# First stage in the order of a written table, small VectorE scalings into padded rows, small doubles zeroed by a bound

## The chip, the cores and the metric

The kernel runs on one core of a Trainium2 chip. A core has a matrix engine (PE, its weight loads PEld), VectorE (DVE), ScalarE (ACT), GpSimd (POOL) and a sync engine (SP) that here only starts transfers. Each engine takes its instructions in program order and waits on semaphores for the others. The metric is the device time of the whole program in microseconds, the median of three runs; beside it stands one profiled execution, from which all durations below come.

## What is computed

There are three layers, one behind the other, over batch 4, sequence 576 and width 512 (8 heads of 64). Only the first and part of the second concern this change.

```python
# layer 1, per batch and head: attention over means of 4 positions, repeated, plus a local band
q_d = q.reshape(B, H, Sd, factor, D).mean(axis=3)        # the same for k and v; factor 4
out_d = sm_attn(q_d, k_d, v_d)                           # softmax attention of 144 x 144
out_up = np.repeat(out_d, factor, axis=2)
mask = np.abs(pos[:, None] - pos[None, :]) < factor      # band of +-3 positions
...                                                      # softmax of the masked scores
return (out_up + out_local).astype(np.float32)
# layer 2: a token mixer and a channel mixer, both relu(x @ w1) @ w2 added to x
h = np.maximum(xt @ w_tok1, 0.0) @ w_tok2
u = x + h.transpose(0, 2, 1)
h2 = np.maximum(u @ w_ch1, 0.0) @ w_ch2
# layer 3: four causal attention experts with a top-2 gate
```

The four weights of layer 2 arrive as 64-bit floats, and the kernel turns them into 32-bit floats on the chip.

## The kernel before, in words

**Stages.** The first stage is layer 1 and the token mixer. The second is the channel mixer: 1440 matmuls into the tile `c`, with the weights converted as it goes. The third is layer 3. The change rewrites the first stage, and one step of the weight conversion that the second stage runs too.

**Units and halves.** Layer 1 is cut into 16 units (batch, pair of heads). A unit has its own steps, each a small function: `q` and `v` load; `qd`, `kd`, `pv` take the sums of four; `sl` (PE) makes the local scores in PSUM, `mx` (DVE) their negated maximum and its scaling by 0.125, `ex` (ACT) ten exponentials with their sums, `rs` (DVE) the reciprocal of the sums, `P` (POOL) the product; `tl` (PE) turns P, `tc` (ACT) copies it out, `ol` (PE) multiplies by v. The pooled attention has the parallel steps `sd`, `md`, `ed`, `rd`, `Pd`, `pdt`, `pc`, `pod`, `oc`. `ad` (DVE) adds the two results into U. After two units a half (batch, half of the width) can run the token mixer: `tx`, `xh`, `xl`, `h`, `hh`, `hl`, `pu`, `ua`. Thirteen weight tiles have the steps `w` (load), `g` (ACT: absolute value of the high word), `t` (ACT: low word), `a`, `f`, `gd` (DVE: shift and mask, join, zero where small), `add` (POOL), `hi` (ACT), `lo` (DVE).

**Order.** The 717 steps of the first stage are emitted in one list, and this list is the order on every engine. Before, `arrange` makes the list while the program is built: it takes, step by step, the one that its table of costs (`COST`) and ranks (`RANK`) puts first. Up to the last unit or weight step the list is emitted alone; the rest (49 steps of the halves) is spread over the first three rounds of the second stage. Two PSUM buffers of two banks serve `sl` and `sd`, so a `sl` or `sd` waits for the `ex` or `ed` two places earlier.

**The small scalings.** Per unit VectorE runs four of them, on 128x10 or 72x4 numbers, all from SBUF to SBUF and each a contiguous row: in `mx` (L463, tile `nmx`), `md` (L493, `nd`), `rs` (L476) and `rd` (L505). ACT's exponentials take `nmx` and `nd` as their bias; POOL's products take `rs` and `rd`.

Of the kernel before, what the change touches and what calls it, by code (L numbers as in the profile page):

```python
# [55 lines left out]
NU, NH, NC = B * NP, 2 * B, 7 + 2 * JG  # L56
COST = dict(
    lq=0.55, qd=0.76, kd=1.45, pv=2.1, sl=1.85, mx=1.0, ex=2.95, rs=0.42, P=1.26, sd=0.65, md=0.95, ed=1.42,
    rd=0.5, Pd=1.14, pdt=0.45, pc=0.7, tl0=0.35, tc0=0.5, tl1=0.23, tc1=0.42, pod=0.55, oc=0.3, ol0=0.55, ad0=0.39,
    ol1=0.8, ad1=0.52, tx0=0.43, xh0=0.62, xl0=0.69, tx1=0.43, xh1=0.62, xl1=0.69, tx2=0.2, xh2=0.38, xl2=0.42,  # L60
    h0=1.7, h1=1.7, hh=0.63, hl=0.66, pu=0.8, ua=0.46, g=0.67, t=0.6, a=0.43, f=0.69, gd=0.68, add=1.26, hi=0.65,
    lo=0.68
)
RANK = dict(
    q=-25.9, v=-9.3, qd=-32.3, kd=45.9, pv=5.7, sl=2.5, mx=-0.7, ex=-25.2, rs=-61.0, P=-3.5, sd=-14.1, md=24.9,
    ed=-0.7, rd=7.4, Pd=-19.3, pdt=-18.8, pc=-3.7, tl=-11.3, tc=-14.7, pod=32.5, oc=-21.4, ol=-13.1, ad=18.2,
    tx=58.0, xh=5.8, xl=-59.2, h=48.8, hh=-16.2, hl=-11.1, pu=63.2, ua=-1.9, w=-38.0, g=44.1, t=9.8, a=11.8,
    f=-11.1, gd=2.5, add=-22.3, hi=5.3, lo=-8.5
)
HELD = dict(b1=ABANKS[0], b2=ABANKS[1], q=3, k=KB, z=KB, vz=VB, vp=1, vd=3, qd=3, kd=3, P=3, Pd=2, PdT=2, PT=2, OdT=2,  # L70
            xh0=1, xh1=1, xh2=1, hh=1, raw=2, w=2)
CONV = (2.8, 11.1, 37.6, 17.7)
SLACK = 0.17


def rank(step, i):
    if step in ("w", "g", "t", "a", "f", "gd", "add", "hi", "lo"):
        c0, cs, d0, ds = CONV
        return (c0 + cs * i if i < 7 else d0 + ds * (i - 7)) + RANK[step]
    return (20 * i + 10 if step in ("tx", "xh", "xl", "h", "hh", "hl", "pu", "ua") else 10 * i) + RANK[step]  # L80


def first_stage():

    ops = {}

    def op(step, i, eng, deps=(), held=(), sub=None, cost=None, after=()):
        cost = COST[step + ("" if sub is None or step + str(sub) not in COST else str(sub))] if cost is None else cost
        ops[step, i, sub] = (eng, cost, deps, held, after, rank(step, i))

    for i in range(NU):
        op("q", i, "SP", cost=[288, 144, 144, 288], after=[("q", i - 1, None)],
           held=[("q", [("sl", i, None), ("qd", i, None)]), ("z", [("sl", i, None)]), ("k", [("kd", i, None)])])
        op("v", i, "SP", cost=[160, 160, 336], after=[("v", i - 1, None)],
           held=[("vz", [("ol", i, 1)]), ("vp", [("pv", i, None)])])
        op("qd", i, "DVE", [("q", i, None)], [("qd", [("sd", i, None)])])
        op("kd", i, "POOL", [("q", i, None)], [("kd", [("sd", i, None)])])
        op("pv", i, "POOL", [("v", i, None)], [("vd", [("pod", i, None)])])
        op("sl", i, "PE", [("q", i, None)], [("b2", [("ex", i, None)])], after=[("tl", i - 3, 1)])
        op("mx", i, "DVE", [("sl", i, None)])  # L100
        op("ex", i, "ACT", [("mx", i, None)], [("P", [("tl", i, 1)])])
        op("rs", i, "DVE", [("ex", i, None)])
        op("P", i, "POOL", [("rs", i, None)])
        op("sd", i, "PE", [("qd", i, None), ("kd", i, None)], [("b2", [("ed", i, None)])], after=[("pdt", i - 2, None)])
        op("md", i, "DVE", [("sd", i, None)])
        op("ed", i, "ACT", [("md", i, None)], [("Pd", [("pdt", i, None)])])
        op("rd", i, "DVE", [("ed", i, None)])
        op("Pd", i, "POOL", [("rd", i, None)])
        op("pdt", i, "PE", [("Pd", i, None)], [("b1", [("pc", i, None)])], after=[("pod", i - 2, None)])
        op("pc", i, "ACT", [("pdt", i, None)], [("PdT", [("pod", i, None)])])  # L110
        op("tl", i, "PE", [("P", i, None)], [("b1", [("tc", i, 0)])], 0, after=[("ol", i - 2, 1)])
        op("tc", i, "ACT", [("tl", i, 0)], [("PT", [("ol", i, 1)])], 0)
        op("tl", i, "PE", [("tl", i, 0)], [("b1", [("tc", i, 1)])], 1)
        op("tc", i, "ACT", [("tl", i, 1), ("tc", i, 0)], [], 1)
        op("pod", i, "PE", [("pc", i, None), ("pv", i, None)], [("b1", [("oc", i, None)])], after=[("ad", i - 2, 1)])
        op("oc", i, "ACT", [("pod", i, None)], [("OdT", [("ad", i, 1)])])
        op("ol", i, "PE", [("tc", i, 1), ("v", i, None), ("pod", i, None)], [("b1", [("ad", i, 0)])], 0)
        op("ad", i, "DVE", [("ol", i, 0), ("oc", i, None)], [], 0)
        op("ol", i, "PE", [("ol", i, 0)], [("b1", [("ad", i, 1)])], 1)
        op("ad", i, "DVE", [("ol", i, 1), ("ad", i, 0)], [], 1)  # L120
    for k in range(NH):
        for g in range(3):
            op("tx", k, "PE", [("ad", 2 * k, 1), ("ad", 2 * k + 1, 1)], [("b1", [("xl", k, g)])], g,
               after=[("h", k - 1, 1)])
            op("xh", k, "ACT", [("tx", k, g)], [(f"xh{g}", [("h", k, 1)])], g)
            op("xl", k, "DVE", [("xh", k, g)], [], g)
        op("h", k, "PE", [("xl", k, g) for g in range(3)] + [("lo", x, None) for x in range(3)],
           [("b1", [("hl", k, None)])], 0, after=[("pu", k - 1, 3)])
        op("h", k, "PE", [("h", k, 0)], [], 1)
        op("hh", k, "ACT", [("h", k, 1)], [("hh", [("pu", k, 3)])])  # L130
        op("hl", k, "DVE", [("hh", k, None)])
        for j in range(4):
            op("pu", k, "PE", [("hl", k, None)] + [("lo", x, None) for x in range(3, 7)] + ([("pu", k, j - 1)] if j else []),
               [("b1", [("ua", k, j)])], j)
            op("ua", k, "DVE", [("pu", k, j)], [], j)
    for x in range(NC):
        z = 1 if x < 2 or x > 6 else 0.5 if x == 2 else 0.6
        op("w", x, "SP", cost=[128 if x == 2 else 512 * z], after=[("w", x - 1, None)],
           held=[("raw", [("f", x, None), ("t", x, None), ("g", x, None)])])
        for step, eng, deps, held in (("g", "ACT", ["w"], [("w", [("lo", x, None), ("hi", x, None)])]),  # L140
                                      ("t", "ACT", ["w", "g"], []), ("a", "DVE", ["w", "g"], []), ("f", "DVE", ["a"], []),
                                      ("gd", "DVE", ["f"], []), ("add", "POOL", ["gd", "t"], []),
                                      ("hi", "ACT", ["add"], []), ("lo", "DVE", ["hi"], [])):
            op(step, x, eng, [(d, x, None) for d in deps], held, cost=COST[step] * z)
    return ops


def arrange(ops):

    end, order, todo = {}, [], dict(ops)  # L150
    free = dict(PE=4.0, ACT=1.0, DVE=3.0, POOL=4.0, SP=0.6)
    held = {k: [] for k in HELD}
    wire, window, warm, busy = 0.0, 0, True, 0.0
    while todo:
        can = []
        for n, (eng, cost, deps, hold, after, r) in todo.items():
            waits = [q for tag, rd in hold if len(held[tag]) >= HELD[tag] for q in held[tag][-HELD[tag]]]
            if any(d not in end for d in deps) or any(d in todo for d in after) or any(q not in end for q in waits):
                continue
            t = max([free[eng]] + [end[d] + (0.09 if ops[d][0] != eng else 0) for d in deps] + [end[q] + 0.09 for q in waits])  # L160
            can.append((t, r, n))
        t, r, n = min(can)
        eng = ops[n][0]
        t, r, n = min((c for c in can if ops[c[2]][0] == eng and c[0] <= t + SLACK), key=lambda c: (c[1], c[0]))
        eng, cost, deps, hold, after, r = todo.pop(n)
        order.append(n)
        if eng == "SP":
            for kb in cost:
                t += 0.5
                wire = max(wire, t + 1.0) + kb * 0.00366  # L170
            free[eng], end[n] = t, wire + 0.9
        else:
            if eng == "PE":
                while t >= (window + 1) * 3.413:
                    warm = busy >= (0.66 if warm else 0.93) * 3.413
                    window, busy = window + 1, 0.0
# [897 lines left out]
```

## Time and profile before

| | us |
|---|---|
| three runs | 713.15, 714.07, 717.11 (median 714.07) |
| the profiled execution | 715.17 |
| its span from the first to the last instruction | 713.4 |
| PE busy in the span | 657.8 (92%) |
| DVE busy | 476.4 (67%) |
| ACT busy | 384.5 (54%) |
| POOL busy | 168.8 (24%) |

The shares are means over three stages that differ: the first stage ends near 190 us, the channel mixer near 508 us. In the first stage PE, DVE, ACT and POOL all work at 64 to 80%. A stretch has to be read by itself.

### The profile page before, as it was taken

The page shows a single profiled execution, that of the slowest core. Times are in us where ns is not written, and L with a number is a line of the kernel's source. Part 1 is how long each engine was busy: PE and PEld are TensorE (multiplying, and loading weights), DVE is VectorE, ACT ScalarE, POOL GpSimd, SP SyncE. Part 2 cuts the span into 40 slices and gives each one's busy share as a digit, 9 for nine tenths or more (in the row PEclk, how much of TensorE's full clock was granted, in tenths as well). Part 3 has the DMA queues.
Part 4 walks back from the last instruction along what each step waited for, and adds up shares of the span by engine and source line. Part 5 has one row for each costly group of instructions (what it writes and reads, how often), then busy time and mean ns, then how long its engine had stood idle before and what let it go on. Part 6 is the DMA issues. An engine that isn't in the chain of part 4 may idle for free.

```text
span 713.4 us, 13279 instructions
## 1 busy us (share of the span) xinstructions
PE 657.8 (92%) x4844; PEld 580.6 (81%) x4844; DVE 476.4 (67%) x1156; ACT 384.5 (54%) x1229; POOL 168.8 (24%) x204
## 2 busy tenths in 40 slices
...
GB/s 251 212 233 183 263 253 179 138 89 40 1 1 29 139 40 60 88 1 5 54 60 1 0 45 16 0 1 1 5 63 26 11 78 50 23 87 34 34 31 103
DMA packets 31760, 52.24 MB, mean 73 GB/s; under 512 B 3728, under 2 KB 16528, under 8 KB 31696
## 3 DMA queue, kind: packets, MB, share of 16 engines
...
q8 instruction: 38, 0.62, 0.4%
...
## 4 chain that ended last, share of the span: by engine, by line
PE 75%; DVE 10%; ACT 8%; POOL 3%; DMA 3%; issue 2%; ACTq 0%; POOLq 0%; DVEq 0%
PE c L222 42%; PE proj L222 7%; PE vp L222 4%; PE o L222 4%; PE wo L222 3%; PE s L222 3%; ACT P L471 3%; PE pt L225 3%; PE h L222 2%; PE pu L222 2%; DMA vp<-in_vp_dram 1%; PE sl L222 1%; DMA qT<-in_qT_dram 1%; ACT PT L901 1%; PE ol L222 1%
## 5 line engine op out<-in xcount | busy, mean ns | idle before, releaser
L257 ACT ACTIVATE hh<-c 128x460 fp32r<-128x460 f32 (+1 forms) x60 | 33.1, 552 | 109.6 <-PE c L222 109.1
L222 PE MATMUL c<-hl,wch 128*128 128x460 f32 (+1 forms) x240 | 89.4, 373 | 0.0
L222 PE MATMUL c<-uh,wcl 128*128 128x460 f32 (+1 forms) x240 | 89.2, 372 | 0.0
L222 PE MATMUL c<-ul,wch 128*128 128x460 f32 (+1 forms) x240 | 89.1, 371 | 0.0
L222 PE MATMUL c<-uh,wch 128*128 128x460 f32 (+1 forms) x240 | 89.1, 371 | 0.0
L222 PE MATMUL c<-hh,wcl 128*128 128x460 f32 (+1 forms) x240 | 89.1, 371 | 0.0
L222 PE MATMUL c<-hh,wch 128*128 128x460 f32 (+1 forms) x240 | 89.0, 371 | 0.0
L266 DVE SCALAR_TENSOR_TENSOR hl<-c,hh 128x460 fp32r<-128x460 f32 (+1 forms) x60 | 38.1, 635 | 59.6 <-ACT hh L257 59.5
L340 POOL TENSOR_TENSOR wc_t<-wc_f,wc_t 128x512 int32<-128x512 int32 x24 | 33.4, 1397 | 175.3 <-ACT wc_t L328 156.4
L680 ACT ACTIVATE uh<-u 128x460 fp32r<-128x460 f32 (+1 forms) x80 | 46.3, 586 | 28.3 <-PE c L222 19.0
L681 DVE TENSOR_TENSOR ul<-u,uh 128x460 fp32r<-128x460 f32 (+1 forms) x80 | 49.8, 634 | 8.0 <-ACT uh L680 8.0
L471 ACT ACTIVATE P<-sl,nmx 128x64 f32<-128x64 f32 x160 | 47.5, 338 | 10.8 <-DVE nmx L463 8.5
L876 ACT ACTIVATE Pc<-Pc,nm 112x576 f32<-112x576 f32 (+4 forms) x80 | 46.8, 588 | 10.0 <-DVE nm L875 9.8
L875 DVE CUSTOM_DVE_ANT_0 Pc<-s,caus 112x576 f32<-112x576 f32 (+4 forms) x80 | 40.8, 517 | 13.2 <-PE s L222 12.0
L222 PEld LDWEIGHTS c<-hh,wch 128*128 128x128 f32 x240 | 45.2, 188 | 5.4
L222 PEld LDWEIGHTS c<-uh,wch 128*128 128x128 f32 x240 | 45.1, 188 | 5.2
L222 PEld LDWEIGHTS c<-uh,wcl 128*128 128x128 f32 x240 | 45.1, 188 | 5.2
L222 PEld LDWEIGHTS c<-ul,wch 128*128 128x128 f32 x240 | 45.1, 188 | 5.2
L222 PEld LDWEIGHTS c<-hh,wcl 128*128 128x128 f32 x240 | 45.1, 188 | 5.1
L222 PEld LDWEIGHTS c<-hl,wch 128*128 128x128 f32 x240 | 45.1, 188 | 5.1
L222 PE MATMUL s<-K,Q 128*112 128x288 f32 (+3 forms) x192 | 42.3, 321 | 3.0 <-DVE Q L268 1.3
L792 POOL MEMSET L<- 116x20 f32 x4 | 0.4, 119 | 170.8 <-DVE u L704 132.5
...
## 6 DMA issues: line engine op xcount, KB each, us to landing
...
```

The source lines that it names most:

```text
L222: behind(nc.tensor.matmul(*a, **kw))
L225: behind(nc.tensor.transpose(*a))
L257: nc.scalar.activation(hi, src, AF.Relu if relu else AF.Copy, **({"scale": scale} if scale else {}))
L266: nc.vector.scalar_tensor_tensor(lo, src, 0.0, h, op0=OP.max, op1=OP.subtract)
L340: nc.gpsimd.tensor_tensor(t, r["f"], t, op=OP.add)
L471: nc.scalar.activation(P[:, t, h], r["sl"][:, bk, j], AF.Exp, bias=r["nmx"][:, bk, j:j + 1], scale=0.125, accum_out=sm[:, t, h:h + 1])
L680: nc.scalar.activation(hi, u, AF.Copy)
L681: getattr(nc, ULO).tensor_tensor(lo, u, hi.bitcast(F32), op=OP.subtract)
L792: nc.gpsimd.memset(ST[b]["L"], 0.0)
L875: nc.vector.tensor_tensor_reduce(pv_, sv, mask, -1.0, 3.0e38, OP.add, OP.min, nm[:nq])
L876: nc.scalar.activation(P[:nq, :n], P[:nq, :n], AF.Exp, bias=nm[:nq], scale=-1.0, accum_out=su[:nq])
L901: nc.scalar.activation(PT[:TQ].rearrange("p (c q) -> p c q", q=S)[:, :m, t * TQ:t * TQ + nq], v[:TQ, :m], AF.Copy)
```

## The change

It has three parts, and 717 steps as before.

1. `arrange` with its costs and ranks is gone. The list of steps stands in the program as a table, `STEPS`; its first words are in the diff below.
2. The four small scalings write rows of 3 of which 2 are used (5 rows for `nmx` and `rs`, 3 rows for `nd` and `rd`), from a contiguous row of 10 or 6. The maxima go into a row of their own first (`nraw`, and one shared `NR`). The sums of `ed` go into three fixed tiles `SR`. Four memsets on POOL fill these tiles once.
3. In the weight conversion `gd` now comes ahead of `a`: it raises the absolute value to at least 2^-15 in place (one input) instead of multiplying the joined word by a comparison (two inputs), and `a` shifts that value instead of the raw high word.

```diff
-    steps = arrange(first_stage())
+    steps = []
+    for word in STEPS.split():
+        step = word.rstrip("0123456789.")
+        i, _, sub = word[len(step):].partition(".")
+        steps.append((step, int(i), int(sub) if sub else None))
...
+STEPS = """
+    q0 kd0 qd0 w0 g0 sl0 q1 gd0 t0 mx0 sd0 a0 w1 f0 md0 v0 ex0 q2 qd1 kd1 sd1 ed0 g1 add0 rs0 hi0 rd0 md1 P0 ed1 gd1
...
-                nc.vector.tensor_scalar(r["a"], r["raw"][:, :, 1], 3, 0x3FFFFFF8, op0=OP.logical_shift_left,
+                nc.vector.tensor_scalar(r["a"], r["g"].bitcast(I32), 3, 0x3FFFFFF8, op0=OP.logical_shift_left,
                                         op1=OP.bitwise_and)
...
-                f = r["f"].bitcast(F32)
-                nc.vector.scalar_tensor_tensor(f, r["g"], 2.0 ** -15, f, op0=OP.is_ge, op1=OP.mult)
+                nc.vector.tensor_scalar(r["g"], r["g"], 2.0 ** -15, None, op0=OP.max)
...
+    NR = pa.tile([72, 6], F32, name="ndraw")
+    SR = [pa.tile([72, 6], F32, name=f"sdm{i}") for i in range(3)]
+    for x in (NR, *SR):
+        nc.gpsimd.memset(x, 1.0)
...
-            nc.vector.tensor_reduce(nmx, r["sl"], axis=AX.X, op=OP.max, negate=True)
-            nc.vector.tensor_scalar_mul(nmx, nmx, 0.125)
+            raw = pa.tile([128, 2 * NT], F32, tag="nraw", bufs=3, name="nraw")
+            nc.vector.tensor_reduce(raw.rearrange("p (b t) -> p b t", b=2), r["sl"], axis=AX.X, op=OP.max, negate=True)
+            r["nmx"] = pa.tile([128, NT, 3], F32, tag="nmx", bufs=3, name="nmx")
+            nc.vector.tensor_scalar_mul(r["nmx"][:, :, :2], raw.rearrange("p (t h) -> p t h", h=2), 0.125)
...
-            rs = r["rs"] = pa.tile([128, NT, 2], F32, tag="rs", bufs=3, name="rs")
-            nc.vector.tensor_scalar(rs, r["sm"], 1e-9, None, op0=OP.add)
+            rs = r["rs"] = pa.tile([128, NT, 3], F32, tag="rs", bufs=3, name="rs")[:, :, :2]
+            nc.vector.tensor_scalar(rs, r["sm"].rearrange("p (t h) -> p t h", h=2), 1e-9, None, op0=OP.add)
...
-            nc.vector.tensor_scalar_mul(nd, nd, 1.0 / 128.0)
+            nc.vector.tensor_scalar_mul(nd[:, :, :2], NR.rearrange("p (h c) -> p h c", c=2), 1.0 / 128.0)
...
-            nc.vector.tensor_scalar(rd, r["sdm"], 1e-9, 4.0, op0=OP.add, op1=OP.mult)
-            nc.vector.reciprocal(rd, rd)
+            nc.vector.tensor_scalar(rd[:, :, :2], SR[i % len(SR)].rearrange("p (c h) -> p c h", h=2), 1e-9, 4.0, op0=OP.add, op1=OP.mult)
+            r["rd"] = rd[:, :2, :2]
+            nc.vector.reciprocal(r["rd"], r["rd"])
...
-        for step in ("w", "g", "t", "a", "f", "gd", "add", "hi", "lo"):
+        for step in ("w", "g", "t", "gd", "a", "f", "add", "hi", "lo"):
```

On SP the loads of the first unit stood behind the first weight before (`wt1_0_raw` is tile 0 of the weights, `qT0_0`, `kz0` and `kT0_0` are q and k of unit 0):

```order
1 L306 DMA wt1_0_raw_128<-in_wt1_dram 128x2x512
2 L409 DMA qT0_0_130<-in_qT_dram 128x576
3 L413 DMA kz0_105<-in_kT_dram 64x576 x2
4 L415 DMA kT0_0_136<-in_kT_dram 128x576
5 L306 DMA wt1_1_raw_138<-in_wt1_dram 128x2x512
```

In the changed kernel the start of SP's list reads:

```order
1 L321 DMA qT0_0_136<-in_qT_dram 128x576
2 L325 DMA kz0_105<-in_kT_dram 64x576 x2
3 L327 DMA kT0_0_142<-in_kT_dram 128x576
4 L214 DMA wt1_0_raw_150<-in_wt1_dram 128x2x512
5 L321 DMA qT0_1_172<-in_qT_dram 128x576
```

The four transfers of unit 0 have moved ahead of the weight.

On POOL the product `P` of unit 0 (tile `P0_0`) stood at the end of this piece before (`vp00`, `vd00` and `vx0` are the sums of v of unit 0, `vz1` and `vx1` are cleared for unit 1):

```order
24 L340 TENSOR_TENSOR wt1_1_t_203<-wt1_1_f_201,wt1_1_t_203 128x512
25 L440 TENSOR_TENSOR vp00_158<-vp00_158 112x3x128
26 L441 TENSOR_TENSOR vd00_247<-vp00_158 112x128
27 L442 TENSOR_TENSOR vx0_111<-vp00_158 64x64
28 L443 TENSOR_TENSOR vx0_111<-vp00_158 48x64
29 L509 TENSOR_TENSOR Pd_252<-Pd_252,rd_269 72x576
30 L399 MEMSET vz1_109 64x640 x2
31 L420 MEMSET vx1_112 112x128
32 L480 TENSOR_TENSOR P0_0_225<-P0_0_225,rs_258 128x640
```

In the changed kernel the same place on POOL reads:

```order
25 L346 TENSOR_TENSOR pool2_228<-kT0_1_178 128x288
26 L347 TENSOR_TENSOR kd_227<-pool2_228 128x144
27 L247 TENSOR_TENSOR wt1_0_t_155<-wt1_0_f_153,wt1_0_t_155 128x512
28 L393 TENSOR_TENSOR P0_0_205<-P0_0_205,rs_247 128x640
29 L423 TENSOR_TENSOR Pd_236<-Pd_236,rd_253 72x576
30 L352 TENSOR_TENSOR vp00_203<-vp00_203 112x3x128
31 L353 TENSOR_TENSOR vd00_292<-vp00_203 112x128
```

`P` of unit 0 has moved ahead of its `Pd`, of the sums of v and of the clearing for unit 1.

On DVE the first maximum (L462, then its scaling) stood behind two weights before (`wt1_0`, `wt1_1`):

```order
8 L428 TENSOR_REDUCE qd_175<-qT0_0_130 128x144
9 L270 TENSOR_TENSOR wt1_0l_197<-wt1_0_t_151,wt1_0h_196 128x512
10 L330 TENSOR_SCALAR wt1_1_a_200<-wt1_1_raw_138 128x512
11 L333 SCALAR_TENSOR_TENSOR wt1_1_f_201<-wt1_1_raw_138,wt1_1_a_200 128x512
12 L462 TENSOR_REDUCE nmx_213<-sl_177 128x10
13 L463 TENSOR_SCALAR nmx_213<-nmx_213 128x10
14 L337 SCALAR_TENSOR_TENSOR wt1_1_f_201<-wt1_1_g_202,wt1_1_f_201 128x512
```

In the changed kernel DVE's list begins so (L244 is `gd`, L374 the maximum, L376 its scaling, L238 `a`, L405 and L406 the maximum and scaling of the pooled scores):

```order
3 L340 TENSOR_REDUCE qd_148<-qT0_0_136 128x144
4 L311 MEMSET kz1_106 64x576 x2
5 L244 TENSOR_SCALAR wt1_0_g_154<-wt1_0_g_154 128x512
6 L374 TENSOR_REDUCE nraw_182<-sl_157 128x10
7 L376 TENSOR_SCALAR nmx_184<-nraw_182 128x5x2
8 L238 TENSOR_SCALAR wt1_0_a_152<-wt1_0_g_154 128x512
9 L241 SCALAR_TENSOR_TENSOR wt1_0_f_153<-wt1_0_raw_150,wt1_0_a_152 128x512
10 L405 TENSOR_REDUCE ndraw_114<-sd_186 72x4
11 L406 TENSOR_SCALAR nd_195<-ndraw_114 72x3x2
```

One `gd` stands ahead of the first maximum now, and the scalings write 5x2 and 3x2 numbers.

## Rows read from the trace of the kernel before

**Rows 1.** Windows: each engine's busy us and count, PEclk, DMA share, GB/s.

```profile
0.00:40.00 40.00, 25.82 (x281) 19.65 (x281) 31.90 (x62) 26.57 (x126) 32.02 (x57) 0.79 0.86 233
40.00:100.00 60.00, 49.19 (x654) 41.60 (x655) 48.95 (x104) 49.62 (x249) 43.12 (x57) 0.94 0.90 230
100.00:160.00 60.00, 48.30 (x589) 41.29 (x583) 54.09 (x102) 41.52 (x171) 41.62 (x49) 0.97 0.52 150
160.00:190.00 30.00, 28.22 (x368) 26.16 (x367) 17.37 (x38) 15.89 (x67) 5.68 (x7) 1.00 0.08 24
...
220.00:520.00 300.00, 297.57 (x1474) 267.90 (x1473) 168.89 (x282) 108.51 (x195) 31.45 (x24) 1.00 0.11 34
```

**Rows 2.** Groups by line and form, VectorE, 0 to 226 us: busy us, mean ns.

```profile
L463 DVE TENSOR_SCALAR nmx<-nmx 128x10 f32<-128x10 f32 x16 | 7.9, 496 | 0.6
...
L337 DVE SCALAR_TENSOR_TENSOR wc_f<-wc_g,wc_f 128x512 f32<-128x512 f32 x10 | 7.1, 715 | 0.7 <-ACT wc_g L326 0.2
L493 DVE TENSOR_SCALAR nd<-nd 72x4 f32<-72x4 f32 x16 | 7.0, 437 | 0.5
...
L505 DVE TENSOR_SCALAR rd<-sdm 72x4 f32<-72x4 f32 x16 | 6.1, 380 | 1.7 <-ACT Pd L500 1.6
...
L476 DVE TENSOR_SCALAR rs<-sm 128x10 f32<-128x10 f32 x16 | 4.0, 248 | 7.5 <-ACT P L471 7.5
```

**Rows 3.** One line each: least, median and greatest duration in ns.

```profile
L463 DVE TENSOR_SCALAR nmx<-nmx x16: 173/256/2280, 11.7 to 162.7; 128x10 f32<-128x10 f32 x16
...
L493 DVE TENSOR_SCALAR nd<-nd x16: 166/307/1371, 13.8 to 157.4; 72x4 f32<-72x4 f32 x16
...
L505 DVE TENSOR_SCALAR rd<-sdm x16: 149/166/1080, 16.4 to 159.2; 72x4 f32<-72x4 f32 x16
...
L476 DVE TENSOR_SCALAR rs<-sm x16: 154/173/1086, 15.0 to 166.5; 128x10 f32<-128x10 f32 x16
...
L477 DVE RECIPROCAL rs<-rs x16: 209/217/218, 16.1 to 166.7; 128x10 f32<-128x10 f32 x16
...
L330 DVE TENSOR_SCALAR wc_a<-wc_raw x24: 409/422/1731, 81.4 to 346.8; 128x512 int32<-128x512 int32 x24
```

**Rows 4.** Timeline of POOL and DVE, 117 to 149 us: start, duration.

```profile
117.73 1.29 POOL L340 TENSOR_TENSOR wc_t<-wc_f,wc_t 128x512 int32<-128x512 int32 x1
118.08 0.98 DVE L463 TENSOR_SCALAR nmx<-nmx 128x10 f32<-128x10 f32 x1
...
146.64 2.28 DVE L463 TENSOR_SCALAR nmx<-nmx 128x10 f32<-128x10 f32 x1
147.54 1.28 POOL L340 TENSOR_TENSOR wc_t<-wc_f,wc_t 128x512 int32<-128x512 int32 x1
```

**Rows 5.** Windows of line 463 alone, then of line 505 alone, 100 to 160 us.

```profile
100.00:160.00 60.00, 3.60 (x4) 0.97 0.52 150
100.00:160.00 60.00, 3.42 (x6) 0.97 0.52 150
```

**Rows 6.** Waits, first stage: us in total, times, longest.

```profile
ACT P L471 <- DVE nmx L463: 8.5, 7, 2.6
...
ACT Pd L500 <- DVE nd L493: 7.1, 5, 2.5
...
PE tl L225 <- POOL P L480: 5.9, 4, 1.8
```

**Rows 7.** Timeline of the first 23 us: SP, PE, ACT, DVE and POOL.

```profile
0.74 0.44 SPq L306 DMA_DIRECT2D wt_raw<-in_wt_dram  x1
7.14 2.43 PE L222 MATMUL sl<-kz,qT 128*64 128x128 f32 x24 [2.03 <-DMA kz<-in_kT_dram]
16.15 0.22 DVE L477 RECIPROCAL rs<-rs 128x10 f32<-128x10 f32 x1
21.57 1.29 POOL L480 TENSOR_TENSOR P<-P,rs 128x640 f32<-128x640 f32 x1
22.92 1.33 PE L225 MATMUL tl<-ident,P 128*128 128x128 f32 x5 [1.83 <-POOL P L480]
```

More of the change, by code (lines that the diff above doesn't have):

```diff
@@ L54 @@
 KB = 3
[L56 to L145, printed above, removed]
@@ L148, in arrange @@
[L148 to L176, printed above, removed]
-                cost *= 1 if warm else 2
-                busy += cost
-            free[eng] = end[n] = t + cost
-        for tag, rd in hold:
-            held[tag].append(rd)
-    return order
```

50 lines of the change are left out of this document (41 added, 9 removed).

## The prediction

> **What bounds the kernel now.** I read the windows first [rows 1]. From 220 to 520 us PE works 297.57 of 300 us, so the channel mixer cannot hide anything: a microsecond that the first stage ends earlier is a microsecond of the whole. In the first 190 us the picture is another. PE works 25.82 + 49.19 + 48.30 + 28.22 = 151.5 us and idles 38.5 us. DVE works 152.3 us, ACT 133.6, POOL 122.4, and the transfers take 122 us (the DMA share of each stretch by its length). No engine is full over the whole stage, so the limit has to be found stretch by stretch. From 100 to 160 us it is DVE: 54.09 of 60 us, with PE next at 48.30. From 40 to 100 us nobody stands out: DVE 48.95, ACT 49.62, PE 49.19, and the DMA share is 0.90. From 0 to 40 us the transfers (0.86), DVE and POOL (32 us each) lead, and PE is granted only 0.79 of its clock.
>
> Then I read which instructions DVE spends that time on [rows 2] and how far one kind varies [rows 3]. The scaling of `nmx` is ten numbers; it takes 173 ns at best and 2280 ns at worst, 496 ns in the mean. The reciprocal on the same ten numbers takes 209 to 218 ns, always. So it is not the size. The timeline shows what the long ones wait for [rows 4]: the scaling that starts at 118.08 ends at 119.06, and the POOL instruction beside it ends at 119.02; the one that starts at 146.64 lasts 2.28 us, to 148.92, and POOL's ends at 148.82. A scaling that meets POOL at work is held until POOL is done. ACT waits for it: 8.5 us for `nmx`, 7.1 us for `nd` [rows 6].
>
> **The change, part by part.**
>
> *Padded rows.* What the holds cost DVE is the busy time less sixteen times the least duration [rows 2, 3]: `nmx` 7.9 - 16 x 0.173 = 5.1 us, `nd` 7.0 - 16 x 0.166 = 4.3, `rd` 6.1 - 16 x 0.149 = 3.7, `rs` 4.0 - 16 x 0.154 = 1.5; together 14.6 us. No row of before shows a scaling that writes 5x2 or 3x2 numbers, so its cost is bounded from both sides: held as now (no gain), or never held, like the reciprocal (14.6 us). I take "never held", because the reciprocal shows that so small an instruction from SBUF to SBUF need not be held at all, and the change alters the one thing about the scalings that could matter, the shape that they write.
>
> [...]
>
> Not all of 14.6 us is freed. If the scaling at 118.08 passes, the `a` that follows it on DVE comes up while POOL still works, and `a` can be held too: 409 ns at best, 1731 at worst [rows 3]. The hold is then handed on. Behind most scalings stands a reduction or an addition from PSUM instead. I take a third as handed on (an estimate), so 9.7 us are freed; the ends are 0 and 14.6.
>
> *`gd`.* Two inputs of 128x512 take 715 ns in the mean [rows 2]. The new form has one input, like `a`, whose median is 422 ns [rows 3]. That is 0.29 us less for eight weights of full size and about half of it for the five smaller ones: 8 x 0.29 + 5 x 0.15 = 3.1 us. It can be held as `a` is, so the ends are 0 and 3.1. `a` keeps its size. In the second stage the same saving lies beside a full PE (DVE works 168.89 of 300 us there [rows 1]) and counts nothing; without that cover it would be 18 weights by 0.29, some 5 us.
>
> *Where DVE's relief reaches the end.* From 100 to 160 us `nmx` and `rd` alone were held for 3.60 - 4 x 0.173 = 2.9 and 3.42 - 6 x 0.149 = 2.5 us [rows 5], 5.4 together. Two thirds of it are 3.6, and half of the `gd` term 1.5, so 5.1 us. DVE falls from 54.1 to 49.0, still over PE's 48.3: all of it counts. From 0 to 100 us there remain (14.6 - 5.4) x 2/3 = 6.1 and 1.6, so 7.7 us. There DVE is 81% busy and the transfers are nearly as full; I count half, 3.9 us, with ends 0 and 7.7.
>
> *The table, at the start.* Unit 0's q and k are sent ahead of the first weight. PE's first scores wait 2.03 us for k [rows 7], and 512 KB at 233 GB/s [rows 1] are 2.2 us, so these 2.0 us go. `rs` of unit 0 is done at 16.15 + 0.22 = 16.37, but `P` starts at 21.57, because on POOL the sums of v, `Pd` and two clearings stand ahead of it; PE's `tl` starts at 22.92 [rows 7]. In the table only the first weight's `add` and two sums of k are ahead, so `P` could start some 5.2 + 2.0 = 7.2 us earlier. `Pd` is now 1.3 us behind it, and the transfers pace the next units (0.86), so I count 2.0 and 1.0 more: 3 us, ends 0 and 7.2.
>
> *The table, elsewhere.* What the order does over 717 steps cannot be summed from rows. The nearest row is PE's wait for `P`, 5.9 us [rows 6], of the kind just seen; I take a third, 2 us. The ends: a loss as in the last rival, and a gain up to PE's idle time that the other terms leave, 38.5 - 12.0 less some 5 us until the first data can be there, 21.5 us.
>
> *Costed at nothing.* The four memsets on POOL run before the first k is there (PE waits for it until 7.14 [rows 7]); without that cover each would cost less than an `rd`, 0.15 us. The shared `NR` is written and read by DVE alone, in order.
>
> Sum: 5.1 + 3.9 + 3.0 + 2.0 = 14.0 us off the profiled execution's 715.17 us (span 713.4 and 1.8 around it), so 701.2. The median of the runs lies 1.1 us below that execution: 700.
>
> **The rivals.**
>
> *The table takes most of PE's idle time.* For it: PE's idle 38.5 us are spread over many short waits, and with DVE relieved the four engines are within a fifth of each other, so a good order could overlap them. Against: the transfers at 0.86 and 0.90 until 100 us. If 12 us of idle remain, 26.5 go: 714 - 26.5 = 687.5.
>
> *The padded rows change nothing,* because 5x2 is held as 10 is, or because the next instruction takes every hold. Then 5.1 becomes 1.5 and 3.9 becomes 0.8: 1.5 + 0.8 + 3.0 + 2.0 = 7.3, so 707. If the transfers also pace everything up to 100 us, only 1.5 + 2.0 remain: 710.5.
>
> *DVE waits for ACT at `gd`; slower.* Before, `a` and `f` needed only the weight from memory, and ACT's `g` was first read behind them. Now `gd` stands first and needs `g`, which stands on ACT behind the exponentials that the table puts ahead of it. DVE is in order, so while `gd` waits, the maxima and scalings behind it wait, and ACT's next exponentials with them. Price: where DVE waits for ACT now (`rs` behind `ex`) it idles 7.5 us in 7 waits [rows 2], 1.1 us each. Thirteen such waits cost 14 us and use up the gain; from 1.35 us each the kernel is slower by more than 0.5%. At 1.6 us each it is 714 - 14 + 20.8 = 721. Against: the table's first `gd` follows its `g` with a transfer in between, and a weight's steps can be set apart.
>
> **How the numbers follow.** A run of three tells about 0.5% (3.6 us) from no change. Forecast 700, between 694 and 707: 0.53. Most of the idle time gone, 682 to 694: 0.18. No gain from the rows, 705 to 712: 0.17, of which 0.05 within 0.5%. DVE behind ACT, 712 to 728: 0.12, of which 0.02 within 0.5%. So faster 0.83, same 0.07, slower 0.10. The range 686 to 712 leaves out some 0.05 below and 0.12 above.
>
> **What would show it.** The four scalings at 0.15 to 0.20 us each, with maxima near their medians; DVE's busy time in the first stage lower by 10 to 15 us; `gd` near 0.42 us; PE's first scores near 5 us and its first `tl` before 18 us; the first matmul into `c` some 14 us before 190. It is wrong if the scalings still reach 1 us, if DVE idles before `gd`, or if the time from the first `c` to the end is not what it was.

## The result, and the profile after

The changed kernel takes 697.6 us (697.15 to 699.02) against 715.59 us before in the same comparison; the ratio is 0.9753, 95% interval 0.9712 to 0.9793. That is 17.7 us less (14.8 to 20.6), where 14.0 were forecast. The time of 700 lies 2.4 us above what was measured.

The same windows of the kernel after (PE, PEld, DVE, ACT, POOL busy, then PEclk, DMA share, GB/s), to be held against [rows 1]:

```profile
0.00:40.00 40.00, 23.80 (x232) 17.59 (x234) 28.03 (x61) 29.12 (x144) 30.59 (x59) 0.87 0.99 243
40.00:100.00 60.00, 55.75 (x816) 46.23 (x817) 49.07 (x121) 55.61 (x281) 50.35 (x67) 1.00 0.99 243
100.00:160.00 60.00, 57.25 (x735) 50.57 (x733) 45.15 (x103) 43.31 (x175) 36.21 (x48) 1.00 0.47 133
...
220.00:520.00 300.00, 296.13 (x1479) 266.68 (x1478) 169.35 (x312) 112.15 (x217) 32.21 (x26) 0.99 0.11 32
```

From 40 to 160 us PE now works 113.0 of 120 us; before it was 97.5. DVE, which led from 100 to 160 us with 54.1, is at 45.2 there, behind PE. The second stage is as it was. So the gain lies where the argument put it, in the first stage, and most of what is left of PE's idle time there stands at the start: 16.2 of the first 40 us.

The scalings, by group and then one line each with least, median and greatest ns (L376 is `nmx`, L406 `nd`, L389 `rs`, L418 `rd`; L244 is `gd`), against [rows 2, 3]:

```profile
L244 DVE TENSOR_SCALAR wc_g<-wc_g 128x512 f32<-128x512 f32 x10 | 7.9, 786 | 1.6 <-ACT wc_g L234 1.6
...
L376 DVE TENSOR_SCALAR nmx<-nraw 128x10 f32<-128x10 f32 x16 | 2.6, 165 | 0.5
L406 DVE TENSOR_SCALAR nd<-ndraw 72x6 f32<-72x6 f32 x16 | 2.5, 155 | 0.6
L389 DVE TENSOR_SCALAR rs<-sm 128x10 f32<-128x10 f32 x16 | 2.4, 151 | 1.8 <-ACT P L384 1.8
L418 DVE TENSOR_SCALAR rd<-sdm 72x6 f32<-72x6 f32 x16 | 2.3, 146 | 2.0 <-ACT Pd L413 2.0
```

```profile
L376 DVE TENSOR_SCALAR nmx<-nraw x16: 164/164/166, 10.2 to 128.0; 128x10 f32<-128x10 f32 x16
L406 DVE TENSOR_SCALAR nd<-ndraw x16: 155/155/156, 12.2 to 125.8; 72x6 f32<-72x6 f32 x16
L389 DVE TENSOR_SCALAR rs<-sm x16: 128/153/165, 14.3 to 134.3; 128x10 f32<-128x10 f32 x16
L418 DVE TENSOR_SCALAR rd<-sdm x16: 123/145/155, 15.1 to 129.3; 72x6 f32<-72x6 f32 x16
```

Not one of 64 is held: `nmx`, which went from 173 to 2280 ns, takes 164 to 166. In the timeline of the kernel before, 30 of the 64 take over 250 ns; all 30 start while POOL works, and 29 of them end 0.02 to 0.10 us after a POOL instruction does. In the changed kernel 52 of the 64 start while POOL works, and the longest of all takes 166 ns. Together they fell from 25.0 to 9.8 us. `gd` is another matter: over the same ten weights it takes 786 ns in the mean, more than the 715 of the old form.

What PE waits for (us, times, longest) until the first matmul into `c`, and the timeline of the start:

```profile
PE sd L130 <- DVE rs L389: 5.1, 1, 5.1
PE sl L130 <- POOL band L151: 3.3, 1, 3.3
PE sd L130 <- POOL kd L347: 3.1, 2, 2.0
PE pod L130 <- ACT PdT L435: 2.9, 1, 2.9
...
PE sl L130 <- ACT P L384: 0.6, 2, 0.3
```

```profile
5.88 2.42 PE L130 MATMUL sl<-kz,qT 128*64 128x128 f32 x24 [1.85 <-DMA kz<-in_kT_dram]
...
14.85 1.26 POOL L393 TENSOR_TENSOR P<-P,rs 128x640 f32<-128x640 f32 x1 [0.88 <-DVE rs L390]
...
18.65 0.55 PE L133 MATMUL tl<-ident,P 128*128 128x128 f32 x3
```

The wait of `tl` for `P` (5.9 us [rows 6]) is off the list. The waits that lead it now are single ones, all in the first 36 us. `sl` starts 1.3 us and `tl` 4.3 us earlier than in [rows 7].

One number sums up the stage, since behind it PE is nearly full (296.13 of 300 us from 220 to 520): the start of the first matmul into `c`. It was 189.6 us, with PE busy for 151.1 and idle for 38.5 of them; it is 170.6, with 146.7 and 23.9. So 14.6 us of the 19.0 are idle time, and 4.4 us are shorter work: the list is the same to eight matmuls, but the granted clock until then is 0.97 where it was 0.93. The rest of the span was 523.8 us in that one execution before and is 526.6 after; the other kernels below, old order or new, have 525.2 to 528.8 there, so I do not put these 3 us down to the change.

### The profile page after: what moved, and what is told of

It reads as the page before. It is cut to its first block, busy times and chain, and to the rows that moved or that the text cites. A ratio compares the mean times of both kernels' runs of the same rounds, so it can differ in the third digit from the quotient of the medians.

```text
span 697.2 us, 13266 instructions
## 1 busy us (share of the span) xinstructions
PE 656.2 (94%) x4844; PEld 577.7 (83%) x4844; DVE 454.1 (65%) x1156; ACT 384.1 (55%) x1229; POOL 162.7 (23%) x208
## 4 chain that ended last, share of the span: by engine, by line
PE 70%; ACT 3%; DVE 3%; issue 1%; DMA 0%; POOL 0%; DVEq 0%; ACTq 0%
PE c L130 43%; PE proj L130 6%; PE vp L130 4%; PE o L130 4%; PE wo L130 3%; PE s L130 3%; PE pt L133 3%; PE pu L130 2%; PE h L130 1%; ACT PT L819 1%; ACT Pc L794 1%; DVE Pc L793 1%; DMA wc_raw<-in_wc_dram 0%; DVE Pc L797 0%; ACT vh L704 0%
## 5 line engine op out<-in xcount | busy, mean ns | idle before, releaser
L598 ACT ACTIVATE uh<-u 128x460 fp32r<-128x460 f32 (+1 forms) x80 | 46.3, 587 | 28.6 <-PE c L130 19.3
L130 PEld LDWEIGHTS c<-hh,wch 128*128 128x128 f32 x240 | 45.2, 188 | 5.4
L793 DVE CUSTOM_DVE_ANT_0 Pc<-s,caus 112x576 f32<-112x576 f32 (+4 forms) x80 | 40.7, 517 | 13.6 <-PE s L130 12.4
```

The source lines that it names most:

```text
L130: behind(nc.tensor.matmul(*a, **kw))
L598: nc.scalar.activation(hi, u, AF.Copy)
L793: nc.vector.tensor_tensor_reduce(pv_, sv, mask, -1.0, 3.0e38, OP.add, OP.min, nm[:nq])
```

## The experiments

The three parts were taken alone and in pairs. Where the old `gd` meets the new table, `a`, `f` and `gd` take the places of `gd`, `a` and `f`; with the new `gd` in the old order it is the other way about.

**The table alone.**

```diff
 # on the kernel before
-    steps = arrange(first_stage())
+    steps = [... for word in STEPS.split()]
+    steps = [({'gd': 'a', 'a': 'f', 'f': 'gd'}.get(n[0], n[0]), *n[1:]) for n in steps]
```

> The new table with the old scalings and the old gd (a, f and gd take the three places that gd, a and f have in the table). Theory 1, that of the prediction: the order is worth 5 us, so some 711; the scalings still reach 1 us and more, 14 us above their least time in the sum. Theory 2: the order is what gives nearly all, 700 to 702, and the freed scalings little. Theory 3: the table was made for scalings that do not wait, so with the old ones it is worth nothing or loses, 714 to 718.

Measured: 710.05 us, ratio 0.9895 (0.9862 to 0.9928), 7.5 us less. The scalings are held as ever:

```profile
L371 DVE TENSOR_SCALAR nmx<-nmx x16: 172/212/1679, 11.1 to 134.3; 128x10 f32<-128x10 f32 x16
```

Theories 2 and 3 fall: the order is worth something without the rows, but less than half of the whole. DVE's work until the first `c` is 152.1 us here, as it was (152.2), so the gain is not DVE's freed time. What changes is whom PE waits for, first in the kernel before, then with the table alone:

```profile
PE pdt L225 <- POOL Pd L509: 7.4, 5, 2.7
PE sl L222 <- ACT P L471: 5.7, 6, 2.0
PE sd L222 <- ACT P L471: 4.9, 2, 4.0
PE sl L222 <- ACT Pd L500: 2.6, 1, 2.6
```

```profile
PE sd L130 <- ACT P L379: 2.6, 2, 2.4
PE sl L130 <- ACT Pd L408: 1.8, 2, 1.0
PE sl L130 <- ACT P L379: 1.0, 1, 1.0
PE tl L133 <- POOL P L388: 0.3, 1, 0.3
```

With the 5.9 us of `tl` [rows 6], PE waited 13.3 us for POOL's two products before and waits 0.3 us now; its waits for the exponentials (lines `P` and `Pd` of ACT) go from 13.2 to 5.4 us. Other waits grow, so not all of this is gained.

**The padded rows alone.**

```diff
 # on the kernel before
-            nc.vector.tensor_scalar_mul(nmx, nmx, 0.125)
+            nc.vector.tensor_scalar_mul(r["nmx"][:, :, :2], raw.rearrange("p (t h) -> p t h", h=2), 0.125)
 # and so for nd, rs and rd
```

> The old order and the old gd with the scalings into padded rows. Theory 1: 14.6 us of holds vanish from the scalings, two thirds are not handed on, and some 7 to 9 us reach the end: 706 to 709. Theory 2: the old order turns the freed time into other waits, within 3 us of before. Both expect the four scalings at 0.12 to 0.17 us each.

Measured: 714.82 us, ratio 0.9951 (0.9923 to 0.9978), 3.5 us less (1.6 to 5.5), half of what theory 1 asked for. The four scalings take 0.15 to 0.17 us in the mean, as both theories had it. Two windows of this kernel say why: the first ends at its first matmul into `c`.

```profile
0.00:186.60 186.60, 153.91 (x1878) 131.67 (x1879) 139.79 (x303) 133.78 (x607) 121.27 (x172) 0.90 0.66 176
...
100.00:160.00 60.00, 51.40 (x641) 44.47 (x638) 51.36 (x106) 43.46 (x184) 41.52 (x50) 0.94 0.51 147
```

DVE's work until the first `c` falls from 152.2 to 139.8 us, so 12.4 us are freed. Nearly nothing is handed on: `a`, `f` and `gd` of 17 weights take 37.3 us in this trace and took 37.0 before. (The scalings' own durations fall by 15.0 us, those of all DVE instructions by 14.2; busy time counts what overlaps once.) But the first `c` comes only 3.0 us earlier. DVE's idle time grew instead, from 37.4 to 46.8 us. PE idles 5.8 us less, and gives back 2.8 of them: it is busy 153.9 us with the same 1878 matmuls, at a granted clock of 0.90 where it was 0.93. The clock is a matter of this execution: over the whole program it had 0.967, while the twelve runs of this kernel had 0.964 to 0.984 and 23 runs of the kernel before 0.962 to 0.983. And the waits that the scalings had caused shrink without going:

```profile
PE tl L225 <- POOL P L486: 5.2, 4, 1.8
...
ACT Pd L506 <- DVE nd L499: 4.5, 5, 1.2
ACT P L477 <- DVE nmx L469: 4.0, 4, 1.4
```

ACT's two waits go from 15.6 to 8.5 us [rows 6]; since no scaling is held any more, I put the rest down to their place in DVE's list, which was not tried by itself. `tl` waits for `P` as before; with the table alone that wait was 0.3 us, so it belongs to the order.

**The new `gd` alone, and the pairs.**

```diff
 # gd alone, on the kernel before
+    steps = [({'a': 'gd', 'f': 'a', 'gd': 'f'}.get(n[0], n[0]), *n[1:]) for n in steps]
-                nc.vector.scalar_tensor_tensor(f, r["g"], 2.0 ** -15, f, op0=OP.is_ge, op1=OP.mult)
+                nc.vector.tensor_scalar(r["g"], r["g"], 2.0 ** -15, None, op0=OP.max)
 # ... and a shifts g, as in the change
```

> The old order and the old scalings, with gd ahead of a (the three steps of a weight keep the places that a, f and gd had). Theory 1: 3 us less DVE work if it is never held, of which 0 to 3 reach the end: 712 to 715. Theory 2: the new gd is held by POOL as often as the old one and waits for ACT besides, so 0 or a loss of 1 to 3 us.

> The changed kernel with the old gd in the places of the table. Theory 1: the sum of table and rows, within 2 us of the changed kernel (some 699). If the new gd carries part of the gain, 702 or more; if it costs time, below 697.

> The changed kernel with the old contiguous scalings. Theory 1 (the parts add up): 7.5 us for the table, 1.4 for gd, so some 9 us below before. Theory 3 (the table was made for this gd): more, 11 us or over. Holds in the scalings are back, some 14 us in the sum over DVE.

> The old order with the padded rows and the new gd. If the parts add up, 3.5 + 1.4 = 5 us below before. If DVE's freed time is worth little because the old order is bound elsewhere, within 4 us of before, with DVE idle longer and PE's waits for ACT as before.

> The changed kernel once more, beside its parts on one chip. It is the yardstick for what the new gd adds to the table and the rows: 14 us below before if it adds nothing, 17 to 18 if the difference seen between two chips is real.

All eight together (us less is one minus the ratio, times 718; first `c` and PE idle until then come from the one profiled execution of each). The kernel before was run anew beside the first four and beside the last four that were measured, with medians of 717.74 and 718.31 us:

| kernel | us | ratio to before | us less | first `c`, us | PE idle until it, us |
|---|---|---|---|---|---|
| before | 718 | 1 | 0 | 189.6 | 38.5 |
| gd | 715.96 | 0.998 (0.9948 to 1.0011) | 1.4 | 191.5 | 35.2 |
| rows | 714.82 | 0.9951 (0.9923 to 0.9978) | 3.5 | 186.6 | 32.7 |
| table | 710.05 | 0.9895 (0.9862 to 0.9928) | 7.5 | 180.7 | 32.6 |
| rows, gd | 710.31 | 0.9891 (0.9845 to 0.9936) | 7.8 | 186.0 | 36.4 |
| table, gd | 706.56 | 0.9834 (0.9792 to 0.9876) | 11.9 | 179.5 | 31.1 |
| table, rows | 703.42 | 0.9806 (0.9775 to 0.9837) | 13.9 | 173.8 | 29.6 |
| all | 698.06 | 0.9731 (0.9686 to 0.9775) | 19.3 | 169.2 | 25.2 |

The three alone make 12.4 us; together they make 17.7 and 19.3. The rows give 3.5 us alone, 6.4 on top of `gd` or of the table and 7.4 on top of both. The table gives 7.5 alone and 10.4 to 11.5 on top of the others. `gd` gives 1.4 alone, which cannot be told from nothing, and 4.3, 4.4 and 5.4 on top of rows, table and both. The intervals are 4 to 6.5 us wide, so a single step of this list is worth little: of the pairs, only table and rows (11.7 to 16.2) clearly leaves out the sum of its parts, 11.0. Rows with `gd` (4.6 to 11.1) still allows 4.9, but not the other theory's "within 4", and table with `gd` (8.9 to 14.9) just allows 8.9. But the direction is the same in all of them, and the whole (16.2 to 22.5) leaves out 12.4: "the parts add up" falls there. Table and rows is 703 and not 699, so the new `gd` carries part of the gain.

For `gd` the traces show where its worth changes. The groups of the three steps of the ten full-size weights that are converted until the first `c`, in the kernel before (`gd` is in [rows 2]), with `gd` alone, with table and rows, and with all:

```profile
L333 DVE SCALAR_TENSOR_TENSOR wc_f<-wc_raw,wc_a 128x512 int32<-128x512 int32 x10 | 7.9, 785 | 0.1
L330 DVE TENSOR_SCALAR wc_a<-wc_raw 128x512 int32<-128x512 int32 x10 | 7.4, 753 | 0.0
```

```profile
L336 DVE TENSOR_SCALAR wc_g<-wc_g 128x512 f32<-128x512 f32 x10 | 9.5, 954 | 2.9 <-ACT wc_g L326 2.9
L333 DVE SCALAR_TENSOR_TENSOR wc_f<-wc_raw,wc_a 128x512 int32<-128x512 int32 x10 | 7.7, 782 | 0.3
L330 DVE TENSOR_SCALAR wc_a<-wc_g 128x512 int32<-128x512 int32 x10 | 5.6, 561 | 0.2
```

```profile
L245 DVE SCALAR_TENSOR_TENSOR wc_f<-wc_g,wc_f 128x512 f32<-128x512 f32 x10 | 9.6, 962 | 0.2
L241 DVE SCALAR_TENSOR_TENSOR wc_f<-wc_raw,wc_a 128x512 int32<-128x512 int32 x10 | 8.7, 872 | 0.1
L238 DVE TENSOR_SCALAR wc_a<-wc_raw 128x512 int32<-128x512 int32 x10 | 8.2, 833 | 2.1 <-DMA wc_raw<-in_wc_dram 2.1
```

```profile
L241 DVE SCALAR_TENSOR_TENSOR wc_f<-wc_raw,wc_a 128x512 int32<-128x512 int32 x10 | 9.0, 913 | 0.2
L238 DVE TENSOR_SCALAR wc_a<-wc_g 128x512 int32<-128x512 int32 x10 | 5.7, 572 | 0.1
L244 DVE TENSOR_SCALAR wc_g<-wc_g 128x512 f32<-128x512 f32 x10 | 4.9, 490 | 1.3 <-ACT wc_g L234 1.3
```

In the old order the new three take 954 + 782 + 561 = 2297 ns and the old three took 785 + 753 + 715 = 2253. The new `gd` is shorter at its best (364 ns in the changed kernel, the old one 673 in the kernel before), but in the old order its mean of 954 ns lies 590 above that, where the old one's lay 42 above its own. In the table's places the new three take 1975 ns and the old three 2667. Over all 17 weights until the first `c` the old three and the new three take 37.0 and 37.3 us in the old order, 37.3 and 35.1 with the rows; in the table 40.1 and 32.6, and with the rows 42.1 and 33.0. So the list decides what the shorter form is worth. It seems to do so by how often the steps are held: in the profile of the changed kernel four of the ten full-size `gd` take 0.81 to 1.74 us, and all four start while POOL works; the six others, at 0.36 to 0.43, start while it does not. For the other kernels only the means are shown, and which places in the list matter was not tried.

**Which shapes are held.**

```diff
 # on the changed kernel
-            r["nmx"] = pa.tile([128, NT, 3], F32, tag="nmx", bufs=3, name="nmx")
+            r["nmx"] = pa.tile([128, 6, 3], F32, tag="nmx", bufs=3, name="nmx")      # 6x2 from a row of 12
-            nc.vector.tensor_scalar_mul(nd[:, :, :2], NR.rearrange("p (h c) -> p h c", c=2), 1.0 / 128.0)
+            nc.vector.tensor_scalar_mul(nd, NR, 1.0 / 128.0)                          # 5 from 5, no gaps
-            nc.vector.tensor_scalar(rs, r["sm"].rearrange("p (t h) -> p t h", h=2), 1e-9, None, op0=OP.add)
+            nc.vector.tensor_scalar(rs, r["sm"][:, :, :2], 1e-9, None, op0=OP.add)    # 5x2 from 5x2, gaps in both
 # ... and the tiles that they read and write, to match
```

> The changed kernel with other shapes in three of the four scalings, one look: nmx writes 6x2 padded from a row of 12, nd writes a contiguous row of 5 from a row of 5, rs writes 5x2 padded from 5x2 padded; rd stays 3x2 padded from a row of 6. [...] If it is the gap in the written row that matters, only nd is held. If it is an odd number of rows, only nmx is held.

One execution, 701.62 us. The four lines, least, median and greatest ns:

```profile
L376 DVE TENSOR_SCALAR nmx<-nraw x16: 174/270/1170, 9.8 to 131.8; 128x12 f32<-128x12 f32 x16
L406 DVE TENSOR_SCALAR nd<-ndraw x16: 168/352/1119, 11.7 to 129.6; 72x5 f32<-72x5 f32 x16
L389 DVE TENSOR_SCALAR rs<-sm x16: 138/366/1242, 13.8 to 138.4; 128x10 f32<-128x10 f32 x16
L418 DVE TENSOR_SCALAR rd<-sdm x16: 123/144/224, 14.6 to 133.5; 72x6 f32<-72x6 f32 x16
```

Three of the four run long here, and neither the gap nor an odd number decides it alone: `nmx` and `rs`, which write rows with gaps, reach 1170 and 1242 ns; `nd` and `rs`, which write 5 from 5 and 5x2 from 5x2, reach 1119 and 1242. Only `rd` stays short (144 ns in the median, 224 at most), which writes 3x2 with gaps from one row of 6. `rs` has now been run in three shapes: ten numbers from ten, without gaps, reached 1086 ns [rows 3]; 5x2 from 5x2, with gaps in both, reaches 1242; 5x2 with gaps from a row of 10 takes 165 at most in the changed kernel. So the shape read counts beside the shape written. What POOL did beside the long ones of this run is not shown, and the seven shapes tried speak for themselves alone: 10 from 10, 4 from 4, 5 from 5, 6x2 from a row of 12 and 5x2 from 5x2 ran long; 5x2 from a row of 10 and 3x2 from a row of 6 did not.

**The start of the table.** Two words were moved back, one in each kernel:

```diff
 # w0_first
-    q0 kd0 qd0 w0 g0 sl0 q1 ...
+    w0 q0 kd0 qd0 g0 sl0 q1 ...
 # p0_late
-    ... rd0 md1 P0 ed1 gd1 sl1 mx1 Pd0 lo0 w2 rd1 pv0 tl0.0 ...
+    ... rd0 md1 ed1 gd1 sl1 mx1 Pd0 lo0 w2 rd1 pv0 P0 tl0.0 ...
```

> The changed kernel with one word of the table moved: the first weight is loaded ahead of unit 0's q and k again. The prediction gave this move 2.0 us; so 2 us slower than the changed kernel (some 700) if it reaches the end, and no change (698) if the transfers behind it pace the stage anyway. PE's first scores start near 7 instead of 5.9 us.

> The changed kernel with P of unit 0 behind Pd and the sums of v on POOL, as before. The prediction gave this 1 us of at most 5. If tl of unit 0 holds up PE's order, PE's third pair of steps comes 3 to 4 us later and the whole is 1 to 4 us slower; if the transfers pace the start, no change.

Measured: 698.65 us (ratio 0.9752, 0.9707 to 0.9798) and 699.34 (0.9756, 0.9715 to 0.9796), against 698.06 of the same kernel without these moves. PE's first scores and its first `tl`, one row from each kernel:

```profile
7.25 2.42 PE L130 MATMUL sl<-kz,qT 128*64 128x128 f32 x24 [3.21 <-DMA kz<-in_kT_dram]
```

```profile
22.07 0.55 PE L133 MATMUL tl<-ident,P 128*128 128x128 f32 x3 [2.16 <-POOL P L393]
```

Both moves do what was said, 1.4 and 3.4 us at their place, but at the end they are 0.6 and 1.3 us by the medians and between 0 and 1.8 by the ratios (0.9731 and 0.9753 for the kernel without them), less than the intervals tell. First `c` comes at 168.6 and 170.0, no later than in the changed kernel (170.6 and 169.2). Each move was undone alone, not both at once.

**Are the transfers the next bound?** The DMA share after the change is 0.99 until 100 us. In one kernel the second load of k is left out and the pooled keys are made from q, so the pooled attention of this kernel is another; in the other they are made from the padded copy of k.

```diff
 # no_kt
-            nc.sync.dma_start(r["k"], kT[b, p])
-            k4 = r["k"].rearrange("p (g r) -> p g r", r=4)
+            k4 = r["q"].rearrange("p (g r) -> p g r", r=4)
 # kd_from_kz: in place of that line and the first addition
+            for h in range(2):
+                hs = slice(64 * h, 64 * h + 64)
+                k4 = kz[hs, h].rearrange("p (g r) -> p g r", r=4)
+                nc.gpsimd.tensor_tensor(a[hs], k4[:, :, 0:2], k4[:, :, 2:4], op=OP.add)
 # ... (the tile of the second load is gone in both)
```

> The changed kernel without the second load of k: it leaves out 288 of 1520 KB a unit, and the pooled keys are made from q, so the result is another. The DMA share of the changed kernel is 0.99 until 100 us. If the transfers are the next bound there, 8 us or more go (690 or less). If the order with DVE, ACT and POOL binds, within 3 us of 698.

> The changed kernel without the second load of k, with the pooled keys made from the padded copy that the local scores read; the result is the reference's. It costs POOL one addition more a unit (some 0.66 us, 10.6 in all, of 118 in the stage). If the transfers bind, it keeps most of what the kernel without the load gains (690 to 694); if POOL binds from 40 to 100 us, it is 2 to 5 us slower than the changed kernel.

Measured: 697.54 us (0.9734, 0.969 to 0.9777) without the load, 700.93 (0.9782, 0.9739 to 0.9825) with the load replaced. The windows of the first:

```profile
0.00:40.00 40.00, 24.63 (x253) 18.61 (x254) 27.07 (x61) 29.86 (x146) 32.21 (x60) 0.87 0.78 210
40.00:100.00 60.00, 54.87 (x816) 46.09 (x813) 52.17 (x123) 55.46 (x278) 52.00 (x70) 1.00 0.70 198
```

A fifth fewer bytes a unit bring the share from 0.99 to 0.78 and 0.70 and leave PE's work in these stretches about where it was. The 8 us that a bound by transfers asked for lie outside the interval, so a share of 0.99 was not a bound; a gain of 3 or 4 us could still hide in it. The second kernel's POOL works 129.1 us until the first `c` (173.7) where it worked 118.0, and is 2.1 to 3.7 us slower than the changed kernel by the ratios, as was expected if POOL's time counts; the intervals overlap, so that is a hint. No version here can be told to beat the changed kernel.

## Why the prediction was right, step by step

- **The bound.** Right in the main: what the first stage ends earlier is gained whole; PE is full behind it. Doubtful in one reading: "from 100 to 160 us it is DVE", so that its relief there "all counts". With the rows alone PE works 3.1 us more in that stretch than before (51.4 for 48.3), near the 3.6 that were counted, though part of it at a lower clock; but DVE idles 8.6 us there where it idled 5.9, and of the 12.4 us freed in the whole stage 3.5 reached the end. A busy share of 90% did not mean that every freed microsecond counts.
- **The rows.** The choice "never held" was right: 5x2 from a row of 10 and 3x2 from a row of 6 take 166 ns at most in 64 scalings, and the rival "5x2 is held as 10 is" falls with that. But the shape written was not the one thing that matters, as the working had it: 5x2 from 5x2 reaches 1242 ns. "A third handed on" was wrong: next to nothing was. Freed work was under-counted (12.4 for 9.7), its way to the end over-counted for the rows alone (3.5 for 6.7, which is 5.1 and 3.9 less 2.3 for `gd`) and about right beside other parts (6.4 to 7.4).
- **`gd`.** Mis-sized. 2.3 of the 9.0 us were its part; alone it gives 1.4 (none to 3.7), with the others 4 to 5. The working set the mean of the old form, 715 ns, against the median of `a`, 422; the mean of `a` over the same ten weights was 753. The new `gd` takes 786 and 490 ns in the mean in two executions of the changed kernel.
- **The table at the start.** The term of 3 us failed: both moves came about (`P` of unit 0 starts at 14.85 where it started at 21.57), but what they give at the end cannot be told from nothing.
- **The table elsewhere.** The term of 2 us was mis-sized most: the table gives 7.5 us alone and over 10 with the rows, and the two moves at the start make up little of it. The traces show where in kind: PE's waits for `P` and `Pd` go and those for the exponentials shrink, and PE's idle time until the first `c` falls from 38.5 to 32.6 and, with rows and `gd`, to 23.9. Which of its 717 places do it was not isolated.
- **The clock.** The sum had no term for it. In the profiled execution 4.4 of the 19.0 us are PE's work done at a higher granted clock (0.97 for 0.93).
- **The rivals.** "Most of PE's idle time goes" came half true: 14.6 of 38.5 us. DVE does wait for ACT's `g` at `gd`, 6.6 us in 5 waits before 171 us, far from the thirteen waits that would have turned the sign. The transfers, feared as a pace until 100 us, gave nothing when a fifth of their bytes went.
- **The signs.** The scalings came as said. DVE's work until the first `c` fell by 20.8 us (152.2 to 131.4) where 10 to 15 were said, the first `c` came 19.0 us earlier where 14 were, and the first `tl` at 18.65 missed "before 18". `gd` near 0.42 us did not come, and DVE idles before it, which had been named a sign of being wrong: in this part the working was wrong.

That the sum of 14.0 came near 17.7 is partly luck, since the errors had both signs: too much for the start, too little for the rest of the order, and no term at all for what the parts give one another, 5 to 7 us. Put on one after the other, table, rows and `gd` gave 7.5, 6.4 and 5.4 us, where the working had 5.0, 6.7 and 2.3.
